# An S5 mixer with an MLP gate: the first block of x in one transfer, the broadcast of D without its hold, and a new order of tasks

## The chip, the cores and the metric

The kernel runs on one core of a Trainium2 chip. The metric is the time of one execution on the device, in microseconds (us), as the median of several runs. All times below are us unless ns is written. TensorE is PE in the profile, and its weight loads PEld; VectorE is DVE, ScalarE ACT, GpSimd POOL; SyncE (SP) only issues transfers here.

## What is computed

x has 2048 rows of 448 (bfloat16). The layer norm xn of x goes two ways, through a diagonal complex state space (S5, 448 states) and through an MLP (448 to 1792 to 448), and the MLP gates the state space:

```python
xn = layernorm(x)
s = 2 * Re(h @ C.T) + xn * Dskip        # h[t] = Lam_bar * h[t-1] + B_bar @ xn[t]
g = silu(gelu(layernorm(xn) @ w1 + b1) @ w2 + b2)
out = x + s * g
# Lam_bar = exp(dt * Lambda), B_bar = (Lam_bar - 1) / Lambda * B, dt = exp(log_dt)
```

## The kernel before, in words

**Tiling.** The 2048 rows are 4 groups g of 2 blocks of 256 rows. A block lies in SBUF as 128 partitions of two rows each, so "par" 0 and 1 mean its even and its odd rows; one partition's two rows are 1792 bytes in a row in memory. The recurrence is folded over such pairs of rows. All of x stays in SBUF (x_all).

**Stages of a group.** Layer norm: statistics (L416/417 for group 0, L388/392 for the others), scales (L419/420 with Ln and Exp on ACT for block 0, L423/424 for block 1, L462 to L472 for whole groups), and the applied forms xn and xn2 (L438 in group 0, L486 on DVE or L487 on ACT). xn and xn2 are transposed, in group 0 by TensorE (L445) and else by transfers on SP's queue. mm1 (mm1_run, L789) multiplies xn2T with w1 into three pairs of PSUM banks, and gelu (L793, ACT) empties them. mm2 (L814) adds up 14 matmuls for each tile of 128 rows in bank 5 or 6 by turns; DVE adds b2 from a broadcast tile b2bc (L817, called o2 in the code and o in the profile) and so frees the bank for the tile after the next. Then silu on ACT (L819, groups 0 and 3) or tanh (L821) with a product on DVE. bu (L717) makes B @ xn in bank 4, copied out by L404. ssm (L729 to L763) does the scan on DVE (L741). ym (L857, L860, L863) makes the output of the state space; DVE and GpSimd add the skip (L834, L869), multiply by the gate (L871, L874) and add x (L877).

**Derived weights.** While group 0 and 1 run, DVE, ACT and GpSimd work out the discretized parameters (L516 to L643): powers and sines of Lambda, the scaled B (lb, L654/656), C times powers (CQ and CZ, L653/654/656) and the direct term M0 (L692 to L708), which TensorE builds from CQ and B. M0's first matmul needs the last CQ.

**The start.** 36 dummy matmuls on a tile of ones (L407) run from 1.1 on, 10 of them behind the arrival of a parameter vector, and two times 5 more between the transposes of block 0. x's first block comes in two transfers (L352/353): even rows on ACT's queue, odd rows on SP's, each 128 pieces of 896 bytes. Block 1 (L336) and w1 in four chunks follow on SP's queue. K = 448 does not divide by 128, so the last 64 rows of w1 lie in both halves of a tile: L349 makes the other half's copy. b2bc (L366) and dbc (L367) are broadcasts of b2 and of D to all partitions, issued from GpSimd's queue; b2bc waits for w1's last chunk, and dbc for b2bc's landing. dbc is then halved (L368 on ACT or L369 on DVE). xd = xn * dbc (L833/834) is its first user. ACT loads the table of Ln and Exp at the start (L313), that of gelu (L428) before the first gelu, that of silu and the sines later, and again that of gelu for group 1.

**What sets the order.** Every step is a task in a list, with an engine, the names that it reads and writes, and sometimes a second engine that could do it ("either"). A list ORDER (L160 to L178), written into the kernel, gives the order in which all tasks are emitted, and so each engine's own order; a list SECOND (L179 to L182) names the tasks that take their second engine. Waits follow from the names: link() finds what each task depends on, emit() (L106 to L151) puts a semaphore wait ahead of a task for each dependency that its engine doesn't know of yet. An engine stands at such a wait, and all that is behind it in its queue stands too.

Of the kernel before, what the change touches and what calls it, by code (L numbers as in the profile page):

```python
# [153 lines left out]
def dram_ap(t, offset, ap):  # L154
    return bass.AP(tensor=t.tensor, offset=offset, ap=ap)
# [2 lines left out]


ORDER = [int(k) for k in """  # L160
# [17 lines left out]
""".split()]  # L178
SECOND = [int(k) for k in """  # L179
46 52 54 55 56 63 65 72 77 78 79 80 84 85 89 90 107 113 131 134 159 162 164 178 185 186 189 190 191 197 223 225 227 229 243 249 250 259 261 329 346  # L180
359 360 370 373 374 393 439 444 463 464 474 475 497 500 502 503 505 507 520 524 569 592 604 607
""".split()]  # L182


# [14 lines left out]
def bass_recurrent_scan__ssm_conv_s5__mixer_channel_mlp__prompt_kernel(  # L199
# [12 lines left out]
    L, D, F = 2048, 448, 1792  # L212
# [5 lines left out]
    with ExitStack() as es:  # L218
        def SB(name, shape, dtype=BF):
            return es.enter_context(nc.sbuf_tensor(name, shape, dtype))  # L220
# [13 lines left out]
        x_all = SB("x_all", [128, NB, 2, D])  # L234
# [9 lines left out]
        dbc = SB("dbc", [128, D])  # L244
# [3 lines left out]
        b2bc = SB("b2bc", [128, D])  # L248
# [54 lines left out]
        with nc.Block():  # L303
# [26 lines left out]
            def ld(eng, o, i, writes, nbytes, prio, reads=(), dur=0.45):  # L330
                kb.dma(eng, o, i, reads=reads, writes=writes, prio=prio, nbytes=nbytes, dur=dur)
# [4 lines left out]
            def ldx(b0, n, prio, reads=(), eng="sp"):  # L336
                ld(eng, x_all[:, b0:b0 + n, :, :], dram_ap(A_x, b0 * 256 * D, [[2 * D, 128], [256 * D, n], [D, 2], [1, D]]),
                   [f"x{b}" for b in range(b0, b0 + n)], n * 256 * D * 2, prio, reads, dur=0.25 + 0.2 * n)
# [10 lines left out]
                kb.either(("dve", lambda e: e.tensor_copy(low, high)), ("act", lambda e: e.activation(low, high, ACT.Copy)), [f"w1_{c}"], [f"w1c_{c}"])  # L349

            S1 = 10 * PINNED
            for par in range(2):  # L352
                ld("sp" if par or not 1 else "act", x_all[:, 0, par, :], dram_ap(A_x, par * D, [[2 * D, 128], [1, D]]), [f"x0p{par}"], 114688, S1)
            ldx(1, 1, S1 + 2)
            ldw1(0, S1 + 1)
            ld("pool", brows[0:3, :], dram_ap(B_b1, 0, [[512, 3], [1, 512]]), ["br0"], 3072, 0, reads=["br"])
# [6 lines left out]
                ld("sp", Bn[ri * 64:ri * 64 + 64, 6, D:896], dram_ap(bm, 384 * D, [[D, 64], [1, D]]), [f"Bn6{ri}"], 57000, S1 + 5, dur=0.55)  # L363
            for c, (a, n) in enumerate(CH):
                ld("sp", w2_sb[:, a:a + n, :], dram_ap(B_w2, a * 128 * D, [[n * D, 128], [D, n], [1, D]]), [f"w2_{c}"], 98000 * n, S1 + 6, dur=0.5 + 0.1 * n)
            ld("pool", b2bc[:], dram_ap(B_b2, 0, [[0, 128], [1, D]]), ["b2bc"], 114688, -50, reads=["sgn3", "w1r_3"])  # L366
            ld("pool", dbc[:], dram_ap(A_Dskip, 0, [[0, 128], [1, D]]), ["dbc"], 114688, -20, reads=["b2bc"])  # L367
            kb.either(("act", lambda e: e.activation(dbc[:], dbc[:], ACT.Copy, scale=0.5), 0.6, 0.2),  # L368
                      ("dve", lambda e: e.tensor_scalar(dbc[:], dbc[:], 0.5, None, op0=ALU.mult), 0.2, 0.12), ["dbc"], ["dbc"], -20)  # L369
            ldx(2, 2, S1 + 7)  # L370
# [635 lines left out]
```

## Time and profile before

| | us |
|---|---|
| median of 3 runs | 155.33 (155.27 to 155.5) |
| the profiled execution's own time | 155.16 |
| its span, first to last instruction | 153.4 |
| outside the span | 1.76 |
| mean granted TensorE clock | 0.998 |

The page of the profile gives busy time by engine, then a chain of work that ended last: followed back from the last instruction, at each step to what released it. Rows of a timeline read "start, length, engine, line, operation, output and input"; the bracket gives the idle time of that engine before the row and what ended it. A releaser marked DMA is a transfer's landing. Rows of DMA issues give the size and the time from issue to landing.

### The profile page before, as it was taken

Reading aid. Unit: us, or ns where it says so; the run is one execution under the profiler, and the core shown is the slowest. Engines: PE = TensorE matmul, PEld = TensorE weight load, DVE = VectorE, ACT = ScalarE, POOL = GpSimd, SP = SyncE. Lnnn points to the kernel's source line nnn. Section 1 sums busy time; section 2 is a strip of 40 time slices with the busy share of each in tenths; the row PEclk is TensorE's granted clock in tenths of the full one; section 3 lists DMA queues with packets and bytes.
Section 4 is the critical chain, followed back from the end, with each engine's and each line's share of the span. In section 5 each row is a group of like instructions: output and inputs, shape, how many; then the busy total and the mean of one; then the engine's idle time right before and its main releaser. Section 6 shows DMA issues by size and latency. Waiting matters only on the chain.

```text
span 153.4 us, 2996 instructions
## 1 busy us (share of the span) xinstructions
PE 148.9 (97%) x1138; PEld 87.6 (57%) x1138; DVE 134.0 (87%) x297; ACT 91.4 (60%) x167; POOL 32.9 (21%) x87
## 2 busy tenths in 40 slices
PE   7999999999999999999999999999999999999992
PEld 7777755454565667654443556764554666555551
DVE  2959989899998899999989998849999848999994
ACT  3598897998871479868765940026389337418010
POOL 5105648133810000020145000022500006000200
PEclk9999999999999999999999999999999999999999
DMA  4899999899889923000003061311900001001022
GB/s 133 244 308 383 225 220 140 146 260 126 154 155 170 135 93 68 0 6 0 0 0 60 4 128 60 68 60 23 142 19 0 0 4 60 0 0 60 4 83 98
DMA packets 31236, 14.73 MB, mean 96 GB/s; under 512 B 24752, under 2 KB 30774, under 8 KB 31222
## 3 DMA queue, kind: packets, MB, share of 16 engines
q1 hardware_dynamic: 30768, 14.14, 41.5%
q0 software_dynamic: 160, 0.23, 0.9%
q8 instruction: 9, 0.15, 0.4%
q10 hardware_dynamic: 294, 0.17, 0.4%
q14 instruction: 5, 0.04, 0.1%
HBM read 6.89 MB, written 1.84 MB: 57 GB/s over the span
## 4 chain that ended last, share of the span: by engine, by line
PE 96%; DVE 1%; issue 0%; DVEq 0%
PE psum L789 29%; PE psum L814 28%; PE psum L717 14%; PE psum L857 12%; PE psum L860 4%; PE psum L407 3%; PE psum L706 3%; PE psum L445 1%; PE psum L863 1%; DVE t L871 1%; DVE tmp L877 0%; PE psum L692 0%; DVEq L303 0%; PE psum L589 0%; DVE ones L306 0%
## 5 line engine op out<-in xcount | busy, mean ns | idle before, releaser
L789 PE MATMUL psum<-xn2T,w_sb 64*128 64x512 bf16 (+1 forms) x462 | 45.5, 346 | 0.4
L814 PE MATMUL psum<-w_sb,gT 128*128 128x448 bf16 x224 | 44.2, 353 | 0.0
L793 ACT ACTIVATE gT<-psum,b1f 128x512 bf16<-128x512 f32 (+1 forms) x66 | 36.6, 622 | 11.0 <-PE psum L789 10.5
L789 PEld LDWEIGHTS psum<-xn2T,w_sb 64*128 64x128 bf16 x462 | 24.2, 110 | 20.6 <-issue 2.6
L814 PEld LDWEIGHTS psum<-w_sb,gT 128*128 128x128 bf16 x224 | 21.8, 98 | 19.7 <-issue 0.2
L717 PE MATMUL psum<-xnT,BT 128*128 128x256 bf16 x196 | 24.0, 273 | 0.0
L717 PEld LDWEIGHTS psum<-xnT,BT 128*128 128x128 bf16 x196 | 18.7, 98 | 5.4 <-issue 1.1
L404 ACT ACTIVATE u_sb<-psum 128x512 bf16<-128x512 f32 (+2 forms) x21 | 9.9, 472 | 18.1 <-PE psum L717 18.0
L741 DVE TENSOR_TENSOR_SCAN s_w<-dk,vs 128x774 f32<-128x774 f32 x8 | 14.1, 1763 | 0.1
L857 PE MATMUL psum<-CZ,h_sb 128*128 128x448 bf16 x56 | 11.9, 353 | 0.0
L817 DVE TENSOR_TENSOR o<-psum,b2bc 128x448 f32<-128x448 f32 x16 | 9.6, 609 | 1.6 <-PE psum L814 1.2
L857 PE MATMUL psum<-CQ,h_sb 128*128 128x448 bf16 (+2 forms) x54 | 10.5, 332 | 0.0
L404 ACT ACTIVATE vs<-s_w 64x256 bf16<-64x256 f32 (+2 forms) x9 | 6.9, 772 | 5.5 <-DVE s_w L741 5.2
L877 POOL TENSOR_TENSOR tmp<-t,x_all 128x448 bf16<-128x448 bf16 x3 | 3.1, 1034 | 32.4 <-DVE t L871 17.8
L486 DVE TENSOR_SCALAR xn_sb<-x_all,lnw 128x448 bf16<-128x448 bf16 (+2 forms) x28 | 9.5, 368 | 0.3
L653 ACT ACTIVATE tmp<-Cr,cw 128x448 f32<-128x448 bf16 (+1 forms) x11 | 7.2, 664 | 3.2 <-DVE CQ L656 3.1
L752 POOL TENSOR_TENSOR ang<-s_w,ang 128x16 f32<-128x16 f32 x3 | 1.6, 535 | 33.6 <-ACT s_w L750 33.6
L487 ACT ACTIVATE xn_sb<-x_all,lnw 128x448 bf16<-128x448 bf16 (+2 forms) x12 | 7.4, 648 | 2.1 <-DVE xn_sb L486 2.0
L857 PEld LDWEIGHTS psum<-CZ,h_sb 128*128 128x128 bf16 x56 | 5.3, 98 | 5.1 <-DVE Cr L869 0.4
L821 ACT ACTIVATE th<-o 128x448 f32<-128x448 f32 x8 | 4.6, 573 | 5.3 <-DVE o L817 5.3
L857 PEld LDWEIGHTS psum<-CQ,h_sb 128*128 128x128 bf16 x54 | 5.1, 98 | 4.1 <-DVE tmp L877 0.4
L860 PE MATMUL psum<-M,xnT 128*128 128x448 bf16 x32 | 7.4, 352 | 0.0
(161 smaller groups left out, 195.5 us busy)
## 6 DMA issues: line engine op xcount, KB each, us to landing
out_dram<-tmp SPq DMA_DIRECT2D x7, 224.0 KB, 1.9
x_all<-in_A_x_dram SPq DMA_DIRECT2D x3, 448.0 KB, 4.3
w_sb<-in_B_w_dram SPq DMA_DIRECT2D x3, 448.0 KB, 7.3
w_sb<-in_B_w_dram SPq DMA_DIRECT2D x3, 384.0 KB, 5.7
vs<-in_A_C_re_dram SPq DMA_DIRECT2D x1, 392.0 KB, 12.2
vs<-in_A_C_im_dram SPq DMA_DIRECT2D x1, 336.0 KB, 10.4
Bn<-in_A_B_im_dram SPq DMA_DIRECT2D x1, 336.0 KB, 10.8
Bn<-in_A_B_re_dram SPq DMA_DIRECT2D x1, 336.0 KB, 10.9
```

The source lines that it names most:

```text
L404: kb.either(("act", [lambda e, o=o, i=i: e.activation(o, i, ACT.Copy) for o, i in pairs]), ("dve", [lambda e, o=o, i=i: e.tensor_copy(o, i ...
L486: on = [("dve", [lambda e, o=o, i=i: e.tensor_scalar(o, i, rs, nb, op0=ALU.mult, op1=ALU.add) for o, i in parts], 0.4, 0.12), ("act", [lam ...
L487: ("act", [lambda e, o=o, i=i: e.activation(o, i, ACT.Identity, bias=nb, scale=rs) for o, i in parts], 0.75, 0.2)]
L653: on = [("act", [lambda e, o=o, i=i, c=c: e.activation(tmp[o, k, :], b[i], ACT.Copy, scale=c[i]) for o, i, c in ps], 0.66 * len(ps), 0.2), ...
L717: fns = [lambda e, r=r, m=m, d=d: e.matmul(psum[:, 4, r * NK:(r + 1) * NK], BT[:, m, d, :], xnT[:, gx, d, :], start=(d == 0), stop=(d == 6 ...
L741: dve(lambda e, so=so, vi=vi: e.tensor_tensor_scan(so, dk[:].rearrange("p i c -> p (i c)"), vi, 0.0, ALU.mult, ALU.add), ["v", "vl", "dk", ...
L789: return lambda e: e.matmul(view(bk[k]), w1_sb[rows, d, fcol(2 * j + k)], rhs[rows, d, :, :], start=not second and n == 0, stop=second and ...
L793: act([lambda e, k=k: e.activation(gT[:, gb, 2 * j + k, :].rearrange("p (r c) -> p r c", r=2)[:, :, cols], view(bk[k]), ACT.Gelu_apprx_tan ...
L814: fns = [lambda e, fi=fi: e.matmul(psum[:, bk, 0:D], gT[:, gb, fi, q * 128:(q + 1) * 128], w2_sb[:, fi, :], start=(fi == 0), stop=(fi == N ...
L817: dve(lambda e: e.tensor_tensor(o2[:, fb, :], psum[:, bk, 0:D], b2bc[:], ALU.add), [f"ps{bk}", "b2bc"], [f"oo{fb}"], 0.62, prio - 76)
L857: fns = [lambda e, k=k: e.matmul(psum[:, bk, c0:c1], h_sb[:, hb, k, k0:k0 + 128], cm[:, k, c0:c1], start=(k == 0), stop=False) for k in ra ...
L860: fns += [lambda e, d=d: e.matmul(psum[:, bk, c0:c1], xnT[:, gx, d, xs], M0[:, d, c0:c1], start=False, stop=(d == 3)) for d in range(4)]
```

## The change

Three edits. (1) The first block of x is one transfer of 224 KB on SP's queue, which writes both names x0p0 and x0p1; ACT's queue issues none of it. The number of tasks goes from 628 to 627. (2) dbc's broadcast depends on the same two names as b2bc's (a constant made by GpSimd, and w1's last chunk) and no longer on b2bc. (3) ORDER and SECOND are new throughout: every engine's order changes, and some tasks change engines. By line and engine, before to after:

| what | before | after |
|---|---|---|
| w1 half copies L349 | DVE 3, others none | DVE 2, ACT 1 |
| dbc halving | DVE 1 | ACT 1 |
| xn2 applies (pairs), groups 1 to 3 | DVE 8, ACT 4 | DVE 4, ACT 8 |
| 128x1024 absolute value L625/626 | DVE 1 | ACT 1 |
| copies out of bank 4 (128x512) | ACT 9, DVE 3 | ACT 12 |
| states' copies, fourth part L404 (128x256, 64x256) | ACT 6, DVE 6 | ACT 12 |
| scalings for CQ, CZ and B, L653/654 (128x448) | ACT 9, DVE 9 | ACT 7, DVE 11 |
| xd products L833/834 | DVE 8 | DVE 5, POOL 3 |
| final adds L877 | DVE 12, POOL 3 | DVE 14, POOL 1 |

The lines of the kernel after are those of before, plus one from L355 on. The diff, with the two lists cut:

```diff
 ORDER = [int(k) for k in """
-20 14 1 0 19 10 95 21 22 15 17 92 96 16 18 25 93 5 23 28 98 97 26 108 3 94 104 27 2 48 91 49 30 50 66 51 4 109 111 6 105 100 99 101 31 106 112 107 102
+18 1 14 2 17 19 0 47 10 16 24 91 15 5 92 3 20 48 93 25 90 94 95 103 104 96 21 105 97 107 49 22 51 26 50 99 106 27 65 66 30 108 23 6 52 55 109 110 98
...
 SECOND = [int(k) for k in """
-46 52 54 55 56 63 65 72 77 78 79 80 84 85 89 90 107 113 131 134 159 162 164 178 185 186 189 190 191 197 223 225 227 229 243 249 250 259 261 329 346
-359 360 370 373 374 393 439 444 463 464 474 475 497 500 502 503 505 507 520 524 569 592 604 607
+23 51 63 64 65 67 72 74 78 82 85 86 87 88 110 112 130 133 158 160 184 187 188 189 190 198 220 222 224 226 228 242 244 246 248 258 269 347 349 358 359
+391 438 440 443 462 463 498 499 510 519 583 606
...
             S1 = 10 * PINNED
-            for par in range(2):
-                ld("sp" if par or not 1 else "act", x_all[:, 0, par, :], dram_ap(A_x, par * D, [[2 * D, 128], [1, D]]), [f"x0p{par}"], 114688, S1)
+            ld("sp", x_all[:, 0, :, :], dram_ap(A_x, 0, [[2 * D, 128], [D, 2], [1, D]]), ["x0p0", "x0p1"], 229376, S1)
+            for par in range(0 if 1 else 2):
+                ld("sp" if par or not 0 else "act", x_all[:, 0, par, :], dram_ap(A_x, par * D, [[2 * D, 128], [1, D]]), [f"x0p{par}"], 114688, S1)
...
-            ld("pool", b2bc[:], dram_ap(B_b2, 0, [[0, 128], [1, D]]), ["b2bc"], 114688, -50, reads=["sgn3", "w1r_3"])
-            ld("pool", dbc[:], dram_ap(A_Dskip, 0, [[0, 128], [1, D]]), ["dbc"], 114688, -20, reads=["b2bc"])
+            ld(("pool", "sp")[0], b2bc[:], dram_ap(B_b2, 0, [[0, 128], [1, D]]), ["b2bc"], 114688, -50, reads=[] if 0 else ["sgn3", "w1r_3"])
+            ld(("pool", "sp")[0], dbc[:], dram_ap(A_Dskip, 0, [[0, 128], [1, D]]), ["dbc"], 114688, -20, reads=[] if 0 else ["sgn3", "w1r_3"])
```

32 rows, old and new, of the table ORDER are left out of this document.

## The prediction

> **What bounds the kernel now.** I read the page first, then the chain of work that ended last in order of time, then the timeline of the start, the windows of TensorE, the DMA issues, and last the waits. Page, busy time and the chain by engine:
>
> ```profile
> PE 148.9 (97%) x1138; PEld 87.6 (57%) x1138; DVE 134.0 (87%) x297; ACT 91.4 (60%) x167; POOL 32.9 (21%) x87
> ...
> PE 96%; DVE 1%; issue 0%; DVEq 0%
> ```
>
> TensorE is the bound, at a granted clock of 0.998. The chain in order of time says where it is not:
>
> ```profile
> 7.47 1.65 PE psum L789 x28
> 9.13 0.11 issue
> ...
> 20.15 10.70 PE psum L814 x56
> 30.85 10.04 PE psum L789 x90
> ...
> 149.21 0.64 DVE t L871
> 149.85 0.02 issue
> 149.87 0.39 DVE tmp L877
> 150.26 0.65 DVE t L871 x2
> 150.91 0.33 DVE tmp L877
> 151.25 0.27 DVEq L303
> ```
>
> From the first matmul of the MLP (7.47) to 149.19 the chain never leaves TensorE for more than 0.11 us. So three places can move the time: the head before 7.47 with the loosely packed first group (to 20.15), a new stall of TensorE in the middle, and the tail of 4.2 us after 149.19. The change leaves the count and shapes of TensorE's instructions alone. The head, on the timeline:
>
> ```profile
> 0.79 0.86 SPq L84 DMA_DIRECT2D x_all<-in_A_x_dram  x2
> 0.80 0.41 ACTq L84 DMA_DIRECT2D x_all<-in_A_x_dram  x1
> ...
> 2.37 1.28 ACT L313 ACT_TABLE_LOAD   x1 [2.37 <-issue]
> ...
> 3.36 1.15 DVE L416 BATCH_NORM_STATS2 lnst<-x_all 128x6 f32<-128x448 bf16 x2 [2.06 <-DMA x_all<-in_A_x_dram]
> ...
> 8.13 1.28 ACT L428 ACT_TABLE_LOAD   x1
> ...
> 9.51 1.93 ACT L793 ACTIVATE gT<-psum,b1f 128x256 bf16<-128x256 f32 x5
> ```
>
> DVE waits 2.06 us for x, but TensorE is full of dummies, transposes and b1 columns from 4.13 to 7.47 (1.25 + 0.31 + 0.83 + 0.28 + 0.28 + 0.39 = 3.34). In the windows of L789 (columns: TensorE busy with its count, weight loads, clock, DMA), the first group takes 11.96 us and the second 11.13 for the same columns:
>
> ```profile
> 7.40:20.10 12.70, 11.96 (x168) 8.85 (x168) 1.00 1.08 297
> 30.80:45.00 14.20, 11.13 (x98) 5.12 (x98) 1.00 0.91 175
> ```
>
> So at most 0.83 + 0.11 us of slack hides in group 0.
>
> **The change, part by part.** All sums go against the profiled execution (155.16; span 153.4, 1.76 outside it), which lies 0.17 below the median 155.33.
>
> *x block 0.* Two transfers of 112 KB become one of 224 KB. The nearest rows, and those of the two broadcasts:
>
> ```profile
> x_all<-in_A_x_dram SPq DMA_DIRECT2D x1, 224.0 KB, 2.8
> ...
> x_all<-in_A_x_dram SPq DMA_DIRECT2D x1, 112.0 KB, 2.5
> x_all<-in_A_x_dram ACTq DMA_DIRECT2D x1, 112.0 KB, 2.7
> b2bc<-in_B_b_dram POOLq DMA_DIRECT2D x1, 112.0 KB, 7.9
> dbc<-in_A_Dskip_dram POOLq DMA_DIRECT2D x1, 112.0 KB, 4.2
> ```
>
> The halves land at 3.34 and 3.52. One transfer issued at 0.79 lands at 3.3 if it takes a half's 2.5, and at 3.6 if it takes block 1's 2.8, which had block 0 ahead of it. I take 3.4. The first statistics then start between 0.05 early and 0.25 late; the second statistics, which started behind the first, lose nothing. TensorE's own 3.34 us from 4.13 stay, since the dummies are still there, so mm1 starts at 7.45 to 7.7.
>
> The Trainium skill ("DMA: Bandwidth & Descriptors", section "Why a DMA increments its semaphore by 16 and not by 1") says that only the full count means landed, so neither half can be used before the whole is there. By it the later end, 3.6, holds for both; the first row's 3.36 shows that today one half is used before the other's 3.52. With 3.6 the sum would grow by up to 0.2.
>
> ACT no longer issues x (0.41), so its vectors and its first table load come about 0.4 earlier; that table waited for nothing and its first user is at 4.68, so it gains nothing.
>
> *ACT's queue in group 0.* One half copy of w1 (0.29 on DVE; 0.60 for a 128x512 copy on ACT) moves to ACT ahead of the gelu table. The table goes from 8.13 to about 8.5, the first gelu from 9.51 to about 9.9. mm1 has three bank pairs, so TensorE waits up to 0.4 there, part of which later slack gives back. Head together: +0.1, from -0.83 (all the slack goes) to +0.5.
>
> *dbc.* The hold cost GpSimd one wait:
>
> ```profile
> POOL dbc L84 <- DMA b2bc<-in_B_b_dram: 0.5, 1, 0.5
> ```
>
> It is 0.45 us, and dbc landed at 25.23 while its scaling ran on DVE at 27.74: the hold hid behind 2.5 us. In the new order dbc stands behind some 20 small GpSimd operations, by their rows at about 18.9 instead of 20.98, and b2bc is out at about 10 (waiting for w1 chunk 3). By 18.9 b2bc has landed even at 7.9, so the removed wait itself is worth nothing. The scaling moves to ACT between the sine activations (needed at about 26.0), and a GpSimd product xd, with parameter products that DVE needs behind it, waits for it. With 4.2 us dbc lands at 23.1, with b2bc's 7.9 at 26.8. I take the first: 0.
>
> *The order.* Every instruction of the middle moves a little. Summed by rows, DVE loses about 4.7 us of occupancy and ACT gains 6.6: four of the eight xn2 pairs that DVE makes (0.60 there, 1.09 on ACT; net over the groups), the 128x1024 absolute value (1.21), the w1 copy, the dbc scaling (0.26) and others go to ACT, three xd (0.39) to GpSimd, two final adds come back to DVE. ACT at 60% has room. What counts is single hand-offs to TensorE:
>
> ```profile
> 24.01 0.59 DVE L817 TENSOR_TENSOR o<-psum,b2bc 128x448 f32<-128x448 f32 x1
> ...
> 27.74 0.26 DVE L369 TENSOR_SCALAR dbc<-dbc 128x448 bf16<-128x448 bf16 x1
> ```
>
> o2 of the first tile ends at 24.6 and frees the bank that the third tile of mm2 takes at 20.15 + 28 x 0.19 = 25.5: slack 0.9. In the new order all four xn2 pairs of group 1 stand ahead of it on DVE; before, two did (22.03 and 23.02), one ran on ACT and one behind o2 (25.74). By the queue's rows it has 20.9 us of work ahead instead of 19.4, so it ends up to 1.5 later (26.1), or 25.1 if DVE idles 1 us less at the start. Stall 0 to 0.6; I take 0.2.
>
> The last CQ ready at 54.73 for M0's matmul at 55.37 (slack 0.64) is laid out again with about 0.2; the add of M0 (70.17 for 70.78) keeps about 0.1; Cr (83.29 for 83.59) about 0.1. Each costs 0 to 0.3, and a stall in front relieves those behind; I take 0 for the three. gelu's second table, ready at about 32.7 instead of 33.56, gains slack only.
>
> *Tail.* DVE is through at 149.02, TensorE at 149.18. One final add (0.32) moves from GpSimd to DVE in front of the last product: slack 0.16 is eaten, +0.1 (0 to 0.2).
>
> Sum: 0.1 + 0 + 0.2 + 0 + 0.1 = **+0.4**, so 155.56 against the profiled run and 155.7 for the median.
>
> **Rivals.** A measurement of this kernel tells about 0.2% (0.31 us) from no change.
>
> *Head packs tighter (faster).* If the first group's gelu no longer holds the banks in the new order, 0.83 goes down by two thirds: -0.55, with the tail +0.1 gives 154.9. For it: 11.96 against 11.13. Against: the table comes later. It decides if the first gelu starts at or before 9.5.
>
> *Nothing reaches TensorE.* All new hand-offs stay inside their slack: 155.3, within 0.2. For it: the dense chain. Against: slack of 0.1 to 0.2 at four places.
>
> *The dbc landing (slower).* ACT reaches the scaling at about 26.0 and stands there until dbc has landed, with the remaining sines, the silus of group 0 and gelu's second table behind it. That table has 0.9 of slack (32.7 for 33.6). If dbc lands after 27, each further us is a us of TensorE: issue at 20 plus 7.9 = 27.9 gives +0.9, with the other terms 156.5. For it: 7.9 for the same kind of transfer. Against: 4.2 for dbc itself.
>
> The Trainium skill ("SBUF — State Buffer", section "SBUF: two separate sides") holds that a transfer issued from GpSimd starves of descriptors while DVE runs in a two-port mode. By it dbc's time would follow DVE's work, and 4.2 against 7.9 for equal transfers fits that; no row here separates it from b2bc's sharing the engines with the weights.
>
> **How the numbers follow.** Forecast (+0.2 to +0.9, median 155.5 to 156.2) 0.45; head tighter 0.22; nothing 0.20; dbc 0.13. About a quarter of the forecast's own case falls within 0.2%, and some of the "nothing" case goes either way: faster 0.24, same 0.29, slower 0.47. The range reaches from 154.8 (head) to 156.5 (dbc); beyond it lie -0.83 undisturbed below and a later dbc or added stalls above, together 2 in 10.
>
> **What would show it.** First statistics at 3.3 to 3.6 and mm1 at 7.45 to 7.7; the gelu table near 8.5; L789 near 12.0 in the first group (rival: 11.4); dbc issued near 18.9 and landed by 24; an "issue" piece or a DVE piece of up to 0.6 in the chain near 25.6 (o2), and small ones near 55, 70 and 83; the last product starting at 149.3 plus what was lost before. The forecast is wrong if TensorE's chain shows a gap of over 0.6 anywhere, if TensorE ends earlier than 149.0, or if ACT waits for dbc.

## The result, and the profile after

| | before | after |
|---|---|---|
| median of 20 runs each | 155.25 | 156.84 |
| lowest and highest | 155.06 to 156.58 | 155.65 to 159.47 |
| profiled execution | 155.16 | 156.1 |
| its span | 153.4 | 154.0 |
| mean granted TensorE clock | 0.998 | 1.000 |

The ratio after to before is 1.0078, with an interval of 1.0058 to 1.0098, so the change costs about 1.2 us (0.0078 x 155.25). The ratio leaves out the two longest executions of the kernel after (158.56 and 159.47), while the medians, which lie 1.6 apart, are over all. Two facts matter more than the median: the executions of the kernel after spread over 3.8 us (1.9 without those two), where 18 of the 20 of before lie within 0.7, and the profiled one is among its quicker ones. Of the 0.94 us between the two profiled executions, 0.6 lies within the span and 0.34 outside it (2.1 against 1.76).

The page of the profile after, busy time and chain by engine:

```profile
PE 148.1 (96%) x1138; PEld 87.3 (57%) x1138; DVE 131.0 (85%) x282; ACT 96.9 (63%) x181; POOL 31.9 (21%) x88
...
PE 69%; DVE 18%; ACT 5%; DMA 4%; issue 2%; SPq 1%; DVEq 0%; ACTq 0%
```

TensorE has the same 1138 matmuls. DVE lost 3 us of busy time, ACT gained 5.5. But the chain, which was 96% TensorE, now runs through DVE, ACT and DMA for more than a quarter of the span: up to 15.56, from 31.52 to 37.02 (the last o2, silu, gelu's second table and four gelus) and from 127.98 to the end, where TensorE itself has no gap of over 0.25. Pieces of that chain in order of time (start, length, what):

```profile
1.72 5.59 DMA w_sb<-in_B_w_dram
...
7.33 0.63 ACT w_sb L349
...
8.55 0.72 DVE xn_sb L439 x2
...
15.23 0.28 DVE w_sb L349
...
15.56 2.94 PE psum L790 x40
...
20.81 10.71 PE psum L815 x56
...
149.87 0.63 DVE t L872
```

The first group begins with a wait for w1's first chunk, which landed at 7.31. The half copy that moved to ACT stands there for it, block 1's Ln and Exp stand behind that copy, and DVE idles 1.00 us before it can apply them at 8.55. From there the chain follows DVE's queue to the last half copy of w1 at 15.23, for which TensorE stands 0.20; mm2 starts at 20.81 instead of 20.15. (The chain counts a matmul from the end of the one before it. By their own starts in the timeline, which the numbers below use, these two are 20.74 and 20.08.) At the other end the last full product starts at 149.87 instead of 149.21. In between DVE has a new idle stretch, at the first statistics of group 2, where it did not wait before (timeline of DVE, before and after):

```profile
33.77 0.61 DVE L388 BATCH_NORM_STATS2 lnst<-x_all 128x6 f32<-128x448 bf16 x1
```

```profile
35.51 1.15 DVE L389 BATCH_NORM_STATS2 lnst<-x_all 128x6 f32<-128x448 bf16 x2 [2.14 <-DMA x_all<-in_A_x_dram]
```

and another one at 95.97, for the store of an output tile (after):

```profile
95.97 0.39 DVE L878 TENSOR_TENSOR tmp<-t,x_all 128x448 bf16<-128x448 bf16 x1 [1.39 <-DMA out_dram<-tmp]
```

Where these two transfers stand on SP's queue (timeline of SP, before and after):

```profile
29.00 0.59 SPq L84 DMA_DIRECT2D x_all<-in_A_x_dram  x1
29.64 1.23 SPq L83 DMA_TRANSPOSE xnT<-xn_sb  x1
30.91 2.78 SPq L83 DMA_TRANSPOSE BT<-Bn  x2
```

```profile
26.71 1.21 SPq L83 DMA_TRANSPOSE Cr<-vs  x1
27.97 0.59 SPq L84 DMA_DIRECT2D Bn<-in_A_B_im_dram  x1
28.60 1.29 SPq L83 DMA_TRANSPOSE Cr<-vs  x1
29.94 1.30 SPq L83 DMA_TRANSPOSE xnT<-xn_sb  x1
31.28 0.58 SPq L84 DMA_DIRECT2D x_all<-in_A_x_dram  x1
...
92.19 1.23 SPq L83 DMA_TRANSPOSE xn2T<-xn_sb  x1
93.47 0.58 SPq L84 DMA_DIRECT2D out_dram<-tmp  x1
```

The load of x for group 2 depends on the first transposed quarter of C (the first "Cr" row), which in the new order stands behind the two xn2 transposes, and three more transfers lie between the two; so the load goes out at 31.28 and lands at 35.49 (33.07 before). The store, whose last add ended by 89.3, stands behind an xn2 transpose that waits for ACT. It went out no earlier before the change (93.94, landed at 95.91), but the next add into its buffer stood only at 99.44 there; in the new order DVE reaches that add at 94.58. So the load of x became late because it goes out later, and the store because its first user comes sooner.

### The profile page after: what moved, and what is told of

The parts are those of the page before. It is cut to its first block, busy times and chain, and to the rows that moved or that the text cites. A ratio compares the mean times of both kernels' runs of the same rounds, so it can differ in the third digit from the quotient of the medians.

```text
span 154.0 us, 2992 instructions
## 1 busy us (share of the span) xinstructions
PE 148.1 (96%) x1138; PEld 87.3 (57%) x1138; DVE 131.0 (85%) x282; ACT 96.9 (63%) x181; POOL 31.9 (21%) x88
## 4 chain that ended last, share of the span: by engine, by line
PE 69%; DVE 18%; ACT 5%; DMA 4%; issue 2%; SPq 1%; DVEq 0%; ACTq 0%
PE psum L790 21%; PE psum L815 21%; PE psum L718 14%; PE psum L858 7%; DMA w_sb<-in_B_w_dram 4%; PE psum L707 3%; PE psum L861 2%; DVE s_w L742 2%; DVE o L818 2%; ACT gT L794 2%; DVE t L872 2%; DVE tmp L878 1%; DVE t L875 1%; ACT L614 1%; ACT vs L405 1%
## 5 line engine op out<-in xcount | busy, mean ns | idle before, releaser
L405 ACT ACTIVATE u_sb<-psum 128x512 bf16<-128x512 f32 (+2 forms) x21 | 10.5, 501 | 12.7 <-PE psum L718 12.5
L405 ACT ACTIVATE vs<-s_w 64x256 bf16<-64x256 f32 (+2 forms) x14 | 7.8, 567 | 15.9 <-DVE s_w L744 11.7
L488 ACT ACTIVATE xn_sb<-x_all,lnw 128x384 bf16<-128x384 bf16 (+2 forms) x21 | 12.2, 629 | 0.1
L875 DVE TENSOR_TENSOR t<-psum,g_sb 128x448 bf16<-128x448 f32 x4 | 2.5, 618 | 8.6 <-PE psum L861 8.6
L389 DVE BATCH_NORM_STATS2 lnst<-x_all 128x6 f32<-128x448 bf16 x12 | 6.9, 611 | 2.1 <-DMA x_all<-in_A_x_dram 2.1
L878 DVE TENSOR_TENSOR tmp<-t,x_all 128x448 bf16<-128x448 bf16 x14 | 6.1, 446 | 1.6 <-DMA out_dram<-tmp 1.4
L753 POOL TENSOR_TENSOR ang<-s_w,ang 128x16 f32<-128x16 f32 x2 | 0.4, 222 | 33.5 <-ACT s_w L751 33.5
L463 POOL TENSOR_SCALAR lnw<-lnmv 128x4 f32<-128x4 f32 x2 | 1.3, 631 | 28.8 <-DVE lnmv L393 28.8
```

Of the source, the lines that this page charges most:

```text
L389: dve([lambda e, b=b, par=par, q=q: e.bn_stats(lnst[:, q, :], x_all[:, 2 * g + b, par, :])], [f"x{2 * g + b}"] , [f"st{q}"], 0.62, prio)
L405: kb.either(("act", [lambda e, o=o, i=i: e.activation(o, i, ACT.Copy) for o, i in pairs]), ("dve", [lambda e, o=o, i=i: e.tensor_copy(o, i ...
L488: ("act", [lambda e, o=o, i=i: e.activation(o, i, ACT.Identity, bias=nb, scale=rs) for o, i in parts], 0.75, 0.2)]
L878: add = lambda e: e.tensor_tensor(o_sb[:, ob, par * D + c0:par * D + c1], t3[:, fb, c0:c1], res, ALU.add)
```

## The experiments

The theories: **H**, the loss lies at the start and the tail, where one profile shows it. **S**, the new order puts transfers on SP's queue behind instructions that wait, DVE then stands in front of their data, and this makes both the loss and the spread (called X where only the load of x was meant). **A, B, C** ask which of the three edits costs anything. Each kernel was timed against the kernel before on the same chip; medians differ by batch (before: 155.38, 155.18, 155.20, 155.15). The third column is the difference of the medians; the intervals are of 95%.

| kernel | median | against before | ratio and interval |
|---|---|---|---|
| x_one | 155.24 | -0.14 | 0.9988 (0.9972 to 1.0004) |
| d_free | 155.35 | -0.03 | 0.9990 (0.9969 to 1.0010) |
| x_two | 157.94 | +2.56 | 1.0129 (1.0079 to 1.0180) |
| d_held | 156.89 | +1.51 | 1.0071 (1.0038 to 1.0103) |
| ct0_first | 156.24 | +1.06 | 1.0049 (1.0024 to 1.0073) |
| tail_copy | 157.54 | +2.36 | 1.0129 (1.0087 to 1.0171) |
| three | 156.69 | +1.51 | 1.0095 (1.0060 to 1.0129) |
| x_late | 159.40 | +4.22 | 1.0226 (1.0175 to 1.0278) |
| store_first | 156.20 | +1.00 | 1.0078 (1.0047 to 1.0109) |
| ct_store | 155.81 | +0.61 | 1.0045 (1.0014 to 1.0076) |
| four | 155.33 | +0.13 | 1.0009 (0.9980 to 1.0037) |
| five | 155.29 | +0.14 | 1.0014 (0.9983 to 1.0045) |

### x_one: the kernel before with the one transfer

```diff
-            for par in range(2):
+            ld("sp", x_all[:, 0, :, :], dram_ap(A_x, 0, [[2 * D, 128], [D, 2], [1, D]]), ["x0p0", "x0p1"], 229376, S1)
+            for par in range(0):
```

> The kernel before with the first block of x as one transfer on SP, and nothing else changed. Theory A (the new order costs the time): 155.2, within 0.2% of before; x lands at 3.4, w1's first chunk may land up to 0.6 later than 6.6, but TensorE needs it at 7.4. Theory B (the one transfer pushes w1's first chunk back and TensorE waits for it): 155.5 to 155.7, with a wait of TensorE for w1 near 7.4 and the first chunk landing at 7.3.

155.24: theory A. x landed at 3.37. w1's first chunk landed at 7.03 and TensorE began mm1 at 7.62 instead of 7.41; by mm2 the old order had made that good (20.10, 20.08 before). In d_free, which has the two transfers of before, the chunk landed at 7.04 and mm1 began at 7.62 as well, so this lateness is not the one transfer's.

### d_free: the kernel before without the hold

```diff
-... ["dbc"], 114688, -20, reads=["b2bc"])
+... ["dbc"], 114688, -20, reads=["sgn3", "w1r_3"])
```

> The kernel before with dbc's broadcast no longer held for b2bc, and nothing else changed: dbc is issued right behind b2bc near 13.5 instead of 20.98. Theory A (the hold hid behind 2.5 us): 155.2, within 0.2%. Theory C (two software transfers at once delay each other or w2): b2bc lands later than 20.7, and with it o2, 155.5 or more only if b2bc lands after 24.0.

155.35, no change. The expectation was wrong on one number: dbc went out at 19.97, not near 13.5, because GpSimd's own order keeps it behind other work. By then b2bc had landed (at 19.33), so the hold would have cost nothing in this execution. The two broadcasts were never under way together, here or in after, so theory C was not tried.

### x_two: the kernel after with two transfers

```diff
-            ld("sp", x_all[:, 0, :, :], dram_ap(A_x, 0, [[2 * D, 128], [D, 2], [1, D]]), ["x0p0", "x0p1"], 229376, S1)
-            for par in range(0 if 1 else 2):
+            for par in range(2):
```

> The kernel after with the first block of x as two transfers again, even rows first on ACT's queue and odd rows on SP's. Theory A (the order of w1 and the other tasks makes the loss): the same as the kernel after, 156.8 plus or minus 0.3. Theory B (the one transfer): about 0.4 less, w1's first chunk at 6.6 and mm1 at 7.4.

Neither: it is slower still. With a half of x ahead of them on ACT's queue, the parameter vectors land later, and the new order has TensorE's parameter matmuls ahead of the ten dummies instead of behind them (timeline of TensorE in x_two):

```profile
6.04 0.21 PE L516 MATMUL psum<-ident,dk 3*128 3x3 bf16 x3 [1.97 <-DMA dk<-in_A_Lambda_re_dram]
```

In the kernel after the same matmuls run at 4.19; here mm1 begins at 8.33 and mm2 at 21.18 (7.71 and 20.74 in after). So in the new order the one transfer looks better than the two, but this is not shown: the intervals overlap (1.0079 to 1.0180 here, 1.0058 to 1.0098 in after), and the profiled execution (156.3) is only 0.2 longer than that of after. What the four longer ones of the six (157.78 to 158.52) lose has no profile.

### d_held: the kernel after with the hold

```diff
-... ["dbc"], 114688, -20, reads=[] if 0 else ["sgn3", "w1r_3"])
+... ["dbc"], 114688, -20, reads=["b2bc"])
```

> The kernel after with dbc held for b2bc's landing again. In the new order dbc stands far behind b2bc (issued at 17.84, b2bc landed at 17.19). Theory A: the same as after, 156.8 plus or minus 0.3, spread from 155.7 to 157.6 as well. Theory C (freeing dbc makes its landing late and varied): 0.5 less than after and a narrower spread. A second profile of this order also shows which rows differ between executions: if dbc's landing moves the end, ACT waits for it at L369.

156.89, the same as after: theory A, C falls. Its profile is of its longest execution (157.62) of what is nearly the same order, and so shows what varies (DVE and TensorE in d_held):

```profile
37.21 1.15 DVE L389 BATCH_NORM_STATS2 lnst<-x_all 128x6 f32<-128x448 bf16 x2 [4.19 <-DMA x_all<-in_A_x_dram]
...
46.80 1.69 PE L718 MATMUL psum<-xnT,BT 128*128 128x256 bf16 x14 [0.50 <-DMA BT<-Bn]
...
97.74 0.39 DVE L878 TENSOR_TENSOR tmp<-t,x_all 128x448 bf16<-128x448 bf16 x1 [2.26 <-DMA out_dram<-tmp]
```

The load of x went out at 31.96 and landed at 37.19. The two transposes of B issued right behind it landed late as well (39.41 and 40.23), and TensorE waits 0.50 for the second of them at 40.37. DVE's scaled B comes later by DVE's own wait, so the later transposes do too, and TensorE waits 0.50 for one at 46.80. At DVE's second wait, for the store, TensorE falls back again: it stands 0.69 for DVE's Cr at 99.89. Against the profile of after it is 0.69 later at 46.8 and 1.75 later at 99.9.

### ct0_first, tail_copy, three: the parts of the new order

ct0_first moves two tasks of ORDER: Ct0 ahead of group 1's two xn2 transposes, and the load of x for group 2 right behind them. tail_copy moves the last half copy of w1 ahead of group 0's scale instructions and gives one final add back to GpSimd. three has both.

```diff
 ORDER, ct0_first
-263 261 249 ... 264 ... 280 214 ... 218
+263 214 261 249 ... 264 218 ... 280
 ORDER and SECOND, tail_copy
-31 155 123 156 136 34
+31 34 155 123 156 136
+603
```

> The kernel after with two tasks moved on SP's queue alone: the first transposed quarter of C goes ahead of group 1's two xn2 transposes, and the load of x for group 2 right behind them, as before the change. Theory X (DVE stands at group 2's statistics until that load has landed, 2.14 us in the profile of after and 4.19 in that of d_held, and this makes both the loss and the spread): the load lands near 32 instead of 35.5 to 37.2, DVE's wait goes, the time falls by 0.8 to 1.2 to 155.7 to 156.0 and the spread to some 0.6. Theory H (the loss lies at the start and the tail, the wait is absorbed): 156.5 to 156.9, with the spread unchanged.

156.24 and a lowest of 155.39: about 0.5 less than after, each against its own before, where 0.8 to 1.2 was expected; the intervals overlap. DVE's wait for x fell to 0.2, but a new one of 1.53 stands at 42.41, for a transposed part of C. The wait for the store stayed (1.91), and the spread with it (155.39 to 157.99): X was at most half right.

> The kernel after with the last half copy of w1 ahead of group 0's ten scale instructions on DVE, and one final add of group 2 back on GpSimd. Theory X: mm2 of group 0 starts up to 0.3 earlier than 20.8 and the tail after TensorE's last full tile is 0.3 shorter, but the median falls by 0.3 to 0.5 only and the spread stays. Theory H: the median falls by 0.6 or more.

> ct0_first and tail_copy together. Theory X: the sum of both, 155.2 to 155.5, no slower than before. Theory H: as tail_copy.

Both misses, at 157.54 and 156.69. mm2 of group 0 started at 19.94 and 20.25 (20.74 after). What the copy is worth is not shown by that, since mm2 started at 20.25 to 20.38 without it too (d_held, ct0_first, store_first, ct_store). The add on GpSimd was put ahead of group 3's last skip product, which DVE needs, and both kernels have this wait (DVE in three):

```profile
146.81 0.62 DVE L870 TENSOR_TENSOR Cr<-psum,xd 128x448 f32<-128x448 f32 x1 [1.45 <-POOL xd L834]
```

That is an error of the edit, not of the change. It was mended in four. The profile of tail_copy (157.9) also shows the faults that it leaves in place: DVE stands 3.65 for the load of x, and TensorE 1.12 for a transpose of B at 46.61.

### x_late: the fault put into the kernel before

```diff
 ORDER of the kernel before: the load of x for group 2
-... 168 ... 194 182 219 ... 167 ... 208 ... 209
+... 168 ... 194 182 ... 167 ... 208 ... 209 219
```

> The kernel before with one task moved: the load of x for group 2 goes on SP's queue behind the xnT transpose and the first two transposes of B, so that it is issued near 33 and lands near 37, as in d_held, while DVE's first statistics of group 2 stand at 33.77. Theory X: DVE idles 3 us there, and the kernel before becomes 0.8 to 1.8 slower with a wider spread. Theory H: within 0.3 of before.

159.40, more than S expected. One load moved past an xnT and two BT transposes, issued at 33.03 instead of 29.00, and nothing else:

```profile
38.70 0.63 DVE L388 BATCH_NORM_STATS2 lnst<-x_all 128x6 f32<-128x448 bf16 x1 [4.46 <-DMA x_all<-in_A_x_dram]
...
54.79 4.51 PE L814 MATMUL psum<-w_sb,gT 128*128 128x448 bf16 x14 [2.45 <-DVE o L817]
```

DVE idles 4.46 us; 16 us later TensorE waits 2.45 for the o2 that stands behind that backlog, and group 2's mm1 begins at 73.13 instead of 68.44. Not all of that is waiting. From 54.9 to 58.3, right behind the wait, the granted clock was 0.50 (1.00 there before), and these 14 matmuls took 4.51 where before they took 2.81. Executions with a mean clock of 1.000 took 158.94 and 159.95, so the loss doesn't need the low clock. The load goes out later here than in after (31.28) and d_held (31.96), and in another order: the run shows that such a fault can cost this much, not what it costs in the new order.

### store_first, ct_store, four, five: the order mended

store_first moves the store of group 0's first tile ahead of the xn2 transpose; ct_store adds ct0_first; four adds the copy, the add on GpSimd and the skip product ahead of it; five adds the load of the real half of B ahead of the xnT transpose that waits for DVE.

```diff
 ORDER, all four
-474 475 ... 431
+474 431 475 ...
 ORDER, four and five
-579 553 ... 580 ... 564 501
+579 553 ... 501 580 ... 564
 ORDER, five
-167 ... 35
+35 167 ...
```

> The kernel after with one task moved on SP's queue: the store of group 0's first output tile goes ahead of group 1's... (group 3's) first xn2 transpose, which waits for ACT. Theory S (DVE's final add at 96 stands for this store's landing, 1.4 to 2.0 us, because the store stood behind the transpose; together with the late load of x this carries the loss into the second half): DVE's wait for the store goes, the store lands near 91, and the median falls by 0.3 to 0.6 to 156.2 to 156.5; the wait for x of group 2 stays. Theory H (start and tail only): unchanged, 156.8.

156.20, lowest 155.77; the wait for the store is gone, that for x stays at 2.1. By the ratio (1.0078) it is not apart from after.

> ct0_first and store_first together: both waits of DVE for a transfer are gone. Theory S: TensorE starts group 3's mm1 at 107.2 to 107.4 as before the change, the median is 155.4 to 155.7, and what is left over before is the tail (0.3). Theory H: 156.2 as ct0_first.

155.81, half of its executions under 155.8: just above what S expected. Group 3's mm1 missed: it began at 107.88 in the profile (an execution of 156.19), not at 107.2 to 107.4. There TensorE stands 0.51 for a transpose of B at 46.30, and DVE has a new wait of 2.5 at 43.41, for a transposed part of C. The spread is only in part gone: the median lies 0.27 above the lowest (1.19 in after, 0.85 in ct0_first, 0.43 in store_first, 0.15 in before of that batch), but two of the twelve took 157.41 and 157.67.

> ct_store with the last half copy of w1 ahead of group 0's scale instructions on DVE, and one final add of group 2 on GpSimd, where this time the last skip product of group 3 goes ahead of that add (in tail_copy and three DVE waited 1.45 us for it). Theory S: the last full product starts at TensorE's end instead of 0.3 behind DVE's queue; 155.0 to 155.3, as before the change or 0.1 to 0.2 faster.

> four with one more task moved on SP's queue: the real half of B is loaded ahead of group 0's xnT transpose that waits for DVE (where it stood before the change), so that it is issued near 13 instead of 19.7 to 20.8. Theory S (the new order leaves transfers behind SP instructions that wait, and DVE and TensorE then stand for their landing): DVE's wait of 1.9 us for it in four goes, the slow executions of four (156.0 to 156.5) become rarer, and the median is 155.0 to 155.2. Against it: nothing changes but noise, 155.3 with the same spread.

155.33 and 155.29 against 155.20 and 155.15. Their intervals end at 1.0037 and 1.0045 and those of after begin at 1.0058: together the moves take back the loss. Neither beats the kernel before, and for five the case against it came out: no change from four but noise. In five the chain is 87% TensorE again, the last product is back in its place, and the store is out 4.6 us sooner than in after (rows of SP and DVE in five):

```profile
28.31 0.58 SPq L84 DMA_DIRECT2D x_all<-in_A_x_dram  x1
...
88.85 0.37 SPq L84 DMA_DIRECT2D out_dram<-tmp  x1
...
149.17 0.63 DVE L872 SCALAR_TENSOR_TENSOR t<-psum,g_sb 128x448 bf16<-128x448 f32 x1
```

four still had a wait of 1.9 for B (landed at 28.61); five has none, but its median says no more than four's. The profile of four is of one of its longer executions (156.45), and there TensorE stood 0.67 at 31.80 for group 1's second xn2 transpose, which landed at 31.66 (28.59 in after, where Ct0 still stood behind it). In five DVE stands 1.9 for a transposed part of C at 42.56, and its profiled execution took 155.14: a wait of DVE is not a loss by itself.

## Why the prediction was right and wrong

The sign was right, the size was a third: +0.4 against some 1.2. By the ratio the time lies at 156.5, the upper end of the range; the median of all executions lies above it. The sign was in part luck: head and tail were of the kind foreseen, but o2's 0.2 was nothing, and another part of the loss (by ct_store some 0.5 to 1.0, with intervals that overlap) came from a place that the sum put at 0.

- **What bounds the kernel**: right. TensorE's work did not change, and what moved the time within the span is at the three places named. Outside the span the sum left 1.76 as it was, and 0.34 of the profiled execution's 0.94 came there. The sums by rows were too high: DVE lost 3.0 us of busy time (4.7 forecast) and ACT gained 5.5 (6.6). One 128x1536 copy of states, three smaller copies and two scalings went from ACT to DVE, which the table of the change doesn't list.
- **x block 0**: right. It landed at 3.39 (3.4 was taken) and x_one shows no effect. The full-count rule of the Trainium skill ("DMA: Bandwidth & Descriptors", section "Why a DMA increments its semaphore by 16 and not by 1") fits the single landing, and its price was nothing. What was missed: ACT's earlier vectors were given no worth. In the new order TensorE waits for them when they are late, as x_two shows.
- **dbc**: right that the hold was worth nothing. The landing was not: 8.1 us and 25.91, not 4.2 and 23.1, and 7.1 to 8.7 in all ten profiles of this order. ACT reached its scaling at 26.15, so the margin was 0.24; ACT waited 0.2 to 0.6 for it in ct0_first, tail_copy and ct_store, and 1.2 in four. Nothing of that shows at the end of after, since ACT idled 0.47 + 1.11 us for DVE between the scaling and gelu's second table. That table was ready at 34.45, not at 32.7, and TensorE's wait for a gelu was 0.20 (at 37.02). The rival's mechanism was there, its price was not. The rule of the Trainium skill ("SBUF — State Buffer", section "SBUF: two separate sides") on starved descriptors was not decided by any run.
- **Head, +0.1**: too small. mm2 started 0.66 later in the profile and 0.17 to 0.30 later in d_held, ct0_first, store_first and ct_store. The half copy on ACT was priced by gelu's table alone. But block 1's Ln and Exp stand behind it too, and DVE idled 0.47 to 1.00 for them in all ten profiles of the new order and in none of the old. The other missing term is the last half copy of w1 behind ten scale instructions on DVE. How much of the 0.66 is the order's is open: w1's first chunk landed at 7.31 there, at 6.4 to 7.3 in the new order and at 6.6 to 7.0 in the old, and x_late, with the old head, began mm2 at 20.48.
- **o2, +0.2**: 0. It ended at 25.70, inside the 25.1 to 26.1 worked out, but TensorE came later as well.
- **The middle, 0**: the step that failed. It counted hand-offs from DVE to TensorE and took 0 to 0.3 for each, and never followed SP's queue, though the order of that queue had changed as much as any. Two transfers land behind their first user there. In the profiled execution slack hid this (TensorE even gained 0.3 between 31.4 and 107.7); in d_held's it did not. Moving the two (ct_store) took back 1.0 of the 1.6 by the medians and 0.5 of the 1.2 by the ratio.
- **Tail, +0.1**: the mechanism was right, the size 0.3: TensorE is 0.36 late at group 3's mm1, and the last product 0.66. DVE has hardly a gap from 143.3 on, so nearly the whole 0.32 of the add comes out at the end.

What stays open: the shares of the waits can't be told apart by time, since the intervals of ct0_first, store_first, ct_store and after overlap; only the sum of all the moves is shown, and it holds parts of H (the copy and the add) with those of S. From ct_store to four these took back another 0.5 by the medians, so H is likely right for a part. And 2.03 to 2.13 us lie outside the span in all 20 executions of the kernel after, against 1.76 in the profiled one of before; 1.69 to 1.76 in those of tail_copy and three, 1.82 to 2.05 in d_held, four and five. No part of the change accounts for it.

## What to carry to other kernels

When an order is replaced, read it for each queue, the transfer queue first: for every transfer, what stands in front of it and what that waits for, against the time its first user stands at. A profile that ends within its slack can still be of a kernel that loses time in most of its executions: ask what margin each landing has, not only whether the engine waited in this one. Putting the suspected fault alone into the good kernel shows in one run whether it can cost anything (x_late); what it costs in the new order took the mended orders, and there only the sum came out.

## What the hardware showed besides

Transposes issued right behind a 448 KB load landed late: the first two BT transposes took 5.05 and 5.98 us in after and 6.81 and 6.37 in d_held, and 3.91 and 3.28 before, where an xnT transpose lay between (that one took 4.33). The load itself took 4.2 in after, 5.2 in d_held and 4.1 before. The Trainium skill says in "DMA: Bandwidth & Descriptors", section "Issuing engines are not separate DMA queues", that transfers run on the same 16 engines and interleave, whichever engine started them; the rows here are all of SP's queue, so no run shows it for two. The broadcast of D (112 KB) took 4.2 to 4.6 us where it was issued at 19.9 to 21.0 (the four profiles of the old order), and 7.1 to 8.7 where it was issued at 17.5 to 18.7; whenever it was issued, it landed between 24.1 and 27.1. What it shares until then was not tried.
